# Grouped-query decode attention with an MLP on one core: unrolled chunks of 8192 keys against engine loops over chunks of 16384 keys

## The chip, the core and the metric

The kernel runs on one core of one Trainium2 chip. The metric is device time in microseconds (us); lower is better. A core has a matrix engine (TensorE, in the profile PE, with its weight loads as PEld), a vector engine (VectorE, DVE), a scalar engine (ScalarE, ACT), GpSimd (POOL) and SyncE (SP), which in this kernel issues nearly all loads. Loads from the chip's main memory into the on-chip memory of 128 partitions are carried out by 16 DMA engines.

## The reference

One token goes through attention over a long cache and, in parallel, through an MLP; both are added to the token. All numbers are float32.

```python
x = A_x                                    # 1 x 1 x 512
xn = layernorm(x)
q = (xn @ wq).reshape(32 heads, 128)       # wq: 512 x 4096
# 8 key/value heads, each used by 4 query heads; 65536 keys of 128 numbers
scores = q . k_cache * 128 ** -0.5
o = softmax(scores) . v_cache
out = x + o.reshape(4096) @ wo + relu(xn @ w1) @ w2    # w1: 512 x 1792, w2: 1792 x 512
```

The two caches have 8 x 65536 x 128 numbers each, 268 MB each. With the weights (wq and wo of 8.4 MB each, w1 and w2 of 3.7 MB each) about 561 MB are read, and 2 KB are written.

## The kernel before

The program is fully unrolled in Python and recorded by a tile framework, which adds the semaphores and assigns buffers out of pools. It goes head by head (`h`, 8 heads with their 4 queries), and within a head first over 8 chunks of 8192 keys (`score_chunk`), then over the same 8 chunks of values (`value_chunk`).

All loads stand in one queue, SyncE's, in the order in which the code is written. A chunk of keys (line 84) is one DMA of 128 rows of 32 KB, one for each partition; a chunk of values (line 93) likewise, but the very last one comes in seven pieces (`LAST`). Keys and values share a pool of four places (`kv`, 32 KB in each partition), so a load waits until the chunk four loads before it has been used. The weights come in pieces of 1 MB from a pool of four (`wpool`, line 77), and their loads stand between the chunks: the part of wq for the next head, w1 and w2 in quarters during the first heads, wo for the head during its values. The last quarter of w2 (line 313) comes in two pieces after the last values.

- Scores (line 166): four matmuls, one for each group of 32 output partitions, make 2048 scores in one bank of PSUM. VectorE transposes that in blocks of 32 x 32 (line 171), ScalarE copies the four used columns of 32 (line 173), and after a chunk VectorE takes its maximum (line 174).
- Softmax (lines 182 to 197): once per head, after all its keys. The maxima go through a transpose on TensorE (line 184), a reduction, a small diagonal matrix (line 188) and a matmul that spreads them to all partitions (line 190), and ScalarE computes the exponentials of the whole head in four instructions, one per query, with their sums.
- Values (line 213): each matmul takes the probabilities of four times 128 keys as weights and 4 x 128 columns of values, into one accumulator per head (`acc_o`); in the last head one times 128.
- Output of a head (lines 246 to 254, then 236): the accumulator is copied, summed over its four blocks with the normalisation (`norm`), and multiplied by this head's part of wo into `acc_y`. This is done while the next head's second chunk of keys is due.
- MLP (lines 268 and 236): pieces of it stand between chunks of the first heads.
- End: after the last values come the output of the last head, the last quarter of w2, an addition of x (line 319) and the store (line 320).

Of the kernel before, what the change touches and what calls it, by code (L numbers as in the profile page):

```python
# [8 lines left out]
F32 = mybir.dt.float32  # L9
# [3 lines left out]
PSUM = bass.MemoryType.PSUM  # L13
# [3 lines left out]
HQ, HKV, DH = 32, 8, 128  # L17
SK = 65536
DFF = 1792
G = HQ // HKV  # L20
# [3 lines left out]
KEYS = CT * TW  # L24
CHUNK = 8192
NCH = SK // CHUNK
TPC = CHUNK // KEYS
NB = CHUNK // P
LAST = {NCH - 1: [16, 16, 8, 8, 8, 4, 4]}
WIDE = 4  # L30
A = D // P
FB = DFF // P
EPS = 1e-5
# [3 lines left out]
def attention_and_mlp_kernel(  # L37
# [10 lines left out]
):  # L48

    nc = tc.nc
    scale = float(DH) ** -0.5

    const = ctx.enter_context(tc.tile_pool(name="const", bufs=1))
    kv = ctx.enter_context(tc.tile_pool(name="kv", bufs=4))  # L60
    wpool = ctx.enter_context(tc.tile_pool(name="wpool", bufs=4))
    work = ctx.enter_context(tc.tile_pool(name="work", bufs=2))
    ps_s = ctx.enter_context(tc.tile_pool(name="ps_s", bufs=3, space=PSUM))
    ps_a = ctx.enter_context(tc.tile_pool(name="ps_a", bufs=1, space=PSUM))
    ps_m = ctx.enter_context(tc.tile_pool(name="ps_m", bufs=2, space=PSUM))


    xT = const.tile([P, A], F32, name="xT")
    nc.scalar.dma_start(xT, x.rearrange("(p a) -> p a", p=P))
    x4 = const.tile([P, P], F32, name="x4")  # L70

    weights = {}

    def load(name, src):
        w = wpool.tile([P, 4, 512], F32, name="w")
        n, m = src.shape[1], src.shape[2]
        nc.sync.dma_start(w[:, :n, :m], src)  # L77
        weights[name] = w

    chunks = {}  # L80

    def load_k(h, n):
        t = kv.tile([P, CHUNK], F32, name="kv")
        nc.sync.dma_start(t, k[h, n])  # L84
        chunks["k", h, n] = t

    def load_v(h, n):
        t = kv.tile([P, CHUNK], F32, name="kv")
        src = v[h, n * CHUNK : (n + 1) * CHUNK, :].rearrange("(p b) d -> p (b d)", p=P)
        b = 0  # L90
        for nb in LAST.get(n, [NB]) if h == HKV - 1 else [NB]:
            cut = slice(b * DH, (b + nb) * DH)
            nc.sync.dma_start(t[:, cut], src[:, cut])
            b += nb
        chunks["v", h, n] = t

    load(("q", 0), wq[0])


    ident = const.tile([P, P], F32, name="ident")  # L100
    make_identity(nc, ident)
    ones = const.tile([P, P], F32, name="ones")
    nc.vector.memset(ones, 1.0)

    sel = const.tile([P, WIDE, G], F32, name="sel")
    places = [ident[:, 32 * c : 32 * c + WIDE * G].rearrange("p (b g) -> p b g", g=G) for c in range(CT)]
    nc.vector.tensor_add(sel, places[0], places[1])
    nc.vector.tensor_add(sel, sel, places[2])
    nc.vector.tensor_add(sel, sel, places[3])
    nc.vector.memset(x4, 0.0)  # L110
    qpad = [const.tile([P, 32], F32, name=f"qpad{i}") for i in range(2)]
    for t in qpad:
        nc.vector.memset(t, 0.0)
    acc_o = [ps_a.tile([P, 512], F32, name=f"acc_o{i}") for i in range(2)]
    for t in acc_o:
        nc.vector.memset(t, 0.0)  # L116
    acc_y = ps_a.tile([P, 512], F32, name="acc_y")
    nc.vector.memset(acc_y[:, :P], 0.0)


    st = const.tile([P, 8], F32, name="st")
    xc = const.tile([P, A], F32, name="xc")
    sq = const.tile([P, A], F32, name="sq")
    xn = const.tile([P, A], F32, name="xn")
    nc.vector.reduce_sum(st[:, 0:1], xT, axis=AX.X)
    pm = ps_m.tile([P, 512], F32, name="pm")
    nc.tensor.matmul(pm[:, 0:1], ones, st[:, 0:1], start=True, stop=True)
    nc.vector.tensor_scalar_mul(st[:, 1:2], pm[:, 0:1], 1.0 / D)
    nc.vector.tensor_scalar(xc, xT, st[:, 1:2], None, op0=ALU.subtract)
    nc.vector.tensor_mul(sq, xc, xc)  # L130
    nc.vector.reduce_sum(st[:, 2:3], sq, axis=AX.X)
    pm = ps_m.tile([P, 512], F32, name="pm")
    nc.tensor.matmul(pm[:, 0:1], ones, st[:, 2:3], start=True, stop=True)
    nc.vector.tensor_scalar(st[:, 3:4], pm[:, 0:1], 1.0 / D, EPS, op0=ALU.mult, op1=ALU.add)
    nc.scalar.activation(st[:, 4:5], st[:, 3:4], AF.Sqrt)
    nc.vector.reciprocal(st[:, 5:6], st[:, 4:5])

    nc.vector.tensor_mul(st[:, 6:7], st[:, 5:6], st[:, 5:6])
    nc.vector.tensor_mul(st[:, 6:7], st[:, 6:7], st[:, 3:4])
    nc.vector.tensor_scalar(st[:, 6:7], st[:, 6:7], -0.5, 1.5, op0=ALU.mult, op1=ALU.add)  # L140
    nc.vector.tensor_mul(st[:, 7:8], st[:, 5:6], st[:, 6:7])
    nc.vector.tensor_scalar_mul(xn, xc, st[:, 7:8])  # L142

    def queries(h):
        w = weights.pop(("q", h))
        pq = ps_m.tile([P, 512], F32, name="pm")
        for g in range(G):
            for a in range(A):
                nc.tensor.matmul(  # L149
                    pq[:, g : g + 1], w[:, a, g * DH : (g + 1) * DH], xn[:, a : a + 1],  # L150
                    start=(a == 0), stop=(a == A - 1),
                )
        nc.vector.tensor_copy(qpad[h % 2][:, :G], pq[:, :G])  # L153

    scores, chunk_max, probs, part_sum = {}, {}, {}, {}

    def score_chunk(h, n):
        t = chunks.pop(("k", h, n))
        if n == 0:
            scores[h] = work.tile([P, NCH * NB, G], F32, name="scores")  # L160
            chunk_max[h] = work.tile([P, G, NCH], F32, name="chunk_max")
        for s in range(TPC):
            pt = ps_s.tile([P, TW], F32, name="pt")
            for c in range(CT):
                lo = (s * CT + c) * TW
                nc.tensor.matmul(  # L166
                    pt[32 * c : 32 * c + 32, :], qpad[h % 2], t[:, lo : lo + TW],
                    start=True, stop=True,
                )
            tr = work.tile([P, SUB, 32], F32, name="tr", bufs=3)  # L170
            nc.vector.transpose(tr.rearrange("p b i -> p (b i)"), pt)  # L171
            b0 = n * NB + s * SUB
            nc.scalar.copy(scores[h][:, b0 : b0 + SUB, :], tr[:, :, :G])  # L173
        nc.vector.reduce_max(  # L174
            chunk_max[h][:, :, n],
            scores[h][:, n * NB : (n + 1) * NB, :].rearrange("p b g -> p g b"),
            axis=AX.X,
        )

    def softmax(h):  # L180
        m = work.tile([P, G], F32, name="m")
        nc.vector.reduce_max(m, chunk_max.pop(h), axis=AX.X)  # L182
        pm = ps_m.tile([P, 512], F32, name="pm")
        nc.tensor.transpose(pm[:G, :P], m, ident)  # L184
        mg = work.tile([G, 1], F32, name="mg")
        nc.vector.reduce_max(mg, pm[:G, :P], axis=AX.X)
        dg = work.tile([G, G], F32, name="dg")
        nc.vector.tensor_scalar(dg, ident[:G, :G], mg, -scale, op0=ALU.mult, op1=ALU.mult)  # L188
        pb = ps_m.tile([P, 512], F32, name="pm")
        nc.tensor.matmul(pb[:, :G], ones[:G, :], dg, start=True, stop=True)  # L190
        bias = work.tile([P, G], F32, name="bias")
        nc.vector.tensor_copy(bias, pb[:, :G])  # L192
        probs[h] = work.tile([P, NCH * NB, G], F32, name="probs")
        part_sum[h] = work.tile([P, G], F32, name="part_sum")
        s = scores.pop(h)
        for g in range(G):
            nc.scalar.activation(  # L197
                probs[h][:, :, g], s[:, :, g], AF.Exp, bias=bias[:, g : g + 1], scale=scale,
                accum_out=part_sum[h][:, g : g + 1],
            )  # L200

    def wide(h):


        return 1 if h == HKV - 1 else WIDE

    def value_chunk(h, n):
        t = chunks.pop(("v", h, n))
        w = wide(h)
        for i in range(NB // w):  # L210
            c = i % CT
            b = n * NB + i * w
            nc.tensor.matmul(  # L213
                acc_o[h % 2][32 * c : 32 * c + w * G, : w * DH],
                probs[h][:, b : b + w, :].rearrange("p b g -> p (b g)"),
                t[:, i * w * DH : (i + 1) * w * DH],
                start=(n == 0 and i < CT), stop=(n == NCH - 1 and i >= NB // w - CT),
            )

    norm = {}  # L220

    def totals(h):

        pm = ps_m.tile([P, 512], F32, name="pm")
        nc.tensor.matmul(pm[:, :G], ones, part_sum.pop(h), start=True, stop=True)  # L225
# [124 lines left out]
```

## Time and profile before

| | |
|---|---|
| median of 3 runs | 1320.74 us (1320.47 to 1320.99) |
| profiled execution, first to last instruction (its span; the profile gives no other time of it) | 1318.7 us |
| median of the runs less this span | 2.0 us |
| read from main memory | 560.99 MB, 425 GB/s over the span |
| granted TensorE clock, mean | 0.752 of full speed |

How to read the profile: busy times are those of each engine and can overlap. The chain that ended last goes back from the last instruction, at each step to what released it. A group's line has the line of code, engine, operation, output and inputs, shapes and count, then busy time and the mean of one in ns, then the idle time just before and what ended it. A line of the timeline has the start, the duration, the instruction and, in brackets, the idle time before it. A line of the windows has the stretch, its length, the busy time of PE, PEld, DVE, ACT and POOL with counts, the granted clock, the mean share of time in which the 16 DMA engines were busy, and GB/s. A line of the DMA queues has packets, MB, and the time of the packets as a share of 16 engines' span. A float32 matmul counts as two instructions on PE and two on PEld.

### The profile page before, as it was taken

Reading aid. Unit: us, or ns where it says so; the run is one execution under the profiler, and the core shown is the slowest. Engines: PE = TensorE matmul, PEld = TensorE weight load, DVE = VectorE, ACT = ScalarE, POOL = GpSimd, SP = SyncE. Lnnn points to the kernel's source line nnn. Section 1 sums busy time; section 2 is a strip of 40 time slices with the busy share of each in tenths; the row PEclk is TensorE's granted clock in tenths of the full one; section 3 lists DMA queues with packets and bytes.
Section 4 is the critical chain, followed back from the end, with each engine's and each line's share of the span. In section 5 each row is a group of like instructions: output and inputs, shape, how many; then the busy total and the mean of one; then the engine's idle time right before and its main releaser. Section 6 shows DMA issues by size and latency. Waiting matters only on the chain.

```text
span 1318.7 us, 12826 instructions
## 1 busy us (share of the span) xinstructions
PE 782.5 (59%) x5702; PEld 261.2 (20%) x5702; DVE 245.4 (19%) x440; ACT 103.5 (8%) x323; POOL 0.7 (0%) x6
## 2 busy tenths in 40 slices
PE   5554676446665466664675556664665644665655
PEld 3211212112121121211211112111121110221244
DVE  3330013300133001330013300233002320023200
ACT  1011000110001100101001110002000120001200
POOL 0000000000000000000000000000000000000000
PEclk9767877877778767667778777767777677777677
DMA  9999999999999999999999999999999999999997
GB/s 399 428 436 430 431 432 425 432 428 432 430 427 430 429 433 429 429 429 430 429 431 432 431 434 431 430 429 429 429 429 435 435 430 431 429 429 430 430 431 289
DMA packets 24646, 561.81 MB, mean 426 GB/s; under 512 B 2696, under 2 KB 3216, under 8 KB 5648
## 3 DMA queue, kind: packets, MB, share of 16 engines
q1 hardware_dynamic: 24448, 561.00, 99.3%
q8 instruction: 44, 0.72, 0.2%
q14 instruction: 10, 0.08, 0.0%
q10 hardware_dynamic: 144, 0.00, 0.0%
HBM read 560.99 MB, written 0.00 MB: 425 GB/s over the span
## 4 chain that ended last, share of the span: by engine, by line
DMA 84%; PE 14%; ACT 0%; DVE 0%; issue 0%; SPq 0%; ACTq 0%; DVEq 0%
DMA kv<-v 43%; DMA kv<-k 42%; PE pt L166 7%; PE acc_o L213 7%; ACT probs L197 0%; PE acc_y L236 0%; DVE acc_o L116 0%; DVE tr L171 0%; SPq L77 0%; DVE chunk_max L174 0%; PE pm L190 0%; PE pm L225 0%; PE pm L252 0%; SPq L84 0%; SPq L287 0%
## 5 line engine op out<-in xcount | busy, mean ns | idle before, releaser
L166 PE MATMUL pt<-kv,qpad 128*32 128x512 f32 x2048 | 361.6, 870 | 233.5 <-DMA kv<-k 233.2
L213 PE MATMUL acc_o<-kv,probs 128*16 128x512 f32 (+1 forms) x2816 | 338.1, 650 | 218.8 <-DMA kv<-v 218.8
L171 DVE STREAM_TRANSPOSE tr<-pt 128x512 f32<-128x512 f32 x256 | 183.5, 717 | 380.4 <-PE pt L166 375.9
L166 PEld LDWEIGHTS pt<-kv,qpad 128*32 128x32 f32 x2048 | 95.9, 152 | 490.6 <-issue 482.8
L213 PEld LDWEIGHTS acc_o<-kv,probs 128*16 128x16 f32 (+1 forms) x2816 | 90.1, 117 | 451.3 <-DMA kv<-v 255.1
L173 ACT COPY scores<-tr 128x64 f32<-128x64 f32 x256 | 62.4, 244 | 1114.2 <-DVE tr L171 1114.2
L153 DVE COPY qpad<-pm 128x4 f32<-128x4 f32 x8 | 1.3, 163 | 398.9 <-PE pm L149 398.9
L174 DVE TENSOR_REDUCE chunk_max<-scores 128x4 f32<-128x256 f32 x64 | 38.5, 601 | 18.6 <-ACT scores L173 18.6
L246 DVE COPY o<-acc_o 128x512 f32<-128x512 f32 (+1 forms) x8 | 5.1, 642 | 190.5 <-PE acc_o L213 190.5
L197 ACT ACTIVATE probs<-scores,bias 128x512 f32<-128x512 f32 x32 | 37.7, 1180 | 18.5 <-DVE bias L192 18.5
L149 PE MATMUL pm<-xn,w 128*128 128x1 f32 x256 | 36.3, 276 | 1.7 <-DVE xn L142 1.7
L149 PEld LDWEIGHTS pm<-xn,w 128*128 128x128 f32 x256 | 35.6, 226 | 8.0 <-issue 6.2
L225 PE MATMUL pm<-part_sum,ones 128*128 128x4 f32 x16 | 4.7, 364 | 42.5 <-ACT probs L197 42.5
L268 PEld LDWEIGHTS pm<-xn,w 128*128 128x128 f32 x112 | 14.0, 206 | 3.5 <-issue 3.5
L268 PE MATMUL pm<-xn,w 128*128 128x1 f32 x112 | 14.3, 262 | 0.0
L225 PEld LDWEIGHTS pm<-part_sum,ones 128*128 128x128 f32 x16 | 4.0, 310 | 43.2 <-ACT probs L197 43.2
L184 PE MATMUL pm<-ident,m 128*4 128x128 f32 x8 | 2.3, 284 | 16.4 <-DVE m L182 16.4
L236 PE MATMUL acc_y<-w,oT 128*1 128x128 f32 x256 | 10.6, 316 | 2.0 <-DVE oT L254 2.0
L252 PE MATMUL pm<-norm,o 128*128 128x4 f32 x58 | 7.8, 256 | 6.2 <-DVE o L246 6.2
L227 DVE RECIPROCAL r<-pm 128x4 f32<-128x4 f32 x8 | 1.5, 183 | 45.9 <-PE pm L225 45.9
L252 PEld LDWEIGHTS pm<-norm,o 128*128 128x128 f32 x58 | 7.1, 191 | 13.9 <-DVE o L246 13.9
L190 PE MATMUL pm<-dg,ones 4*128 4x4 f32 x16 | 4.3, 335 | 5.0 <-DVE dg L188 5.0
(47 smaller groups left out, 45.1 us busy)
## 6 DMA issues: line engine op xcount, KB each, us to landing
kv<-k SPq DMA_DIRECT2D x64, 4096.0 KB, 34.3
kv<-v SPq DMA_DIRECT2D x63, 4096.0 KB, 35.1
w<-wq SPq DMA_DIRECT2D x8, 1024.0 KB, 40.3
w<-wo SPq DMA_DIRECT2D x8, 1024.0 KB, 35.2
w<-w SPq DMA_DIRECT2D x6, 1024.0 KB, 34.8
kv<-v SPq DMA_DIRECT2D x2, 1024.0 KB, 26.4
kv<-v SPq DMA_DIRECT2D x3, 512.0 KB, 29.6
w<-w SPq DMA_DIRECT2D x1, 512.0 KB, 34.4
```

The costliest lines, as they stand in the source:

```text
L149: nc.tensor.matmul(pq[:, g : g + 1], w[:, a, g * DH : (g + 1) * DH], xn[:, a : a + 1], start=(a == 0), stop=(a == A - 1),)
L166: nc.tensor.matmul(pt[32 * c : 32 * c + 32, :], qpad[h % 2], t[:, lo : lo + TW], start=True, stop=True,)
L171: nc.vector.transpose(tr.rearrange("p b i -> p (b i)"), pt)
L173: nc.scalar.copy(scores[h][:, b0 : b0 + SUB, :], tr[:, :, :G])
L174: nc.vector.reduce_max(chunk_max[h][:, :, n], scores[h][:, n * NB : (n + 1) * NB, :].rearrange("p b g -> p g b"), axis=AX.X,)
L197: nc.scalar.activation(probs[h][:, :, g], s[:, :, g], AF.Exp, bias=bias[:, g : g + 1], scale=scale, accum_out=part_sum[h][:, g : g + 1],)
L213: nc.tensor.matmul(acc_o[h % 2][32 * c : 32 * c + w * G, : w * DH], probs[h][:, b : b + w, :].rearrange("p b g -> p (b g)"), t[:, i * w * ...
L225: nc.tensor.matmul(pm[:, :G], ones, part_sum.pop(h), start=True, stop=True)
L236: nc.tensor.matmul(acc_y[32 * c : 32 * c + 1, :P], lhsT, row[:, c * P : (c + 1) * P], start=first[0], stop=last,)
L246: nc.vector.tensor_copy(o[:, :n, :].rearrange("p b d -> p (b d)"), acc_o[h % 2][:, : n * DH])
L252: nc.tensor.matmul(pm[:, :G], o[:, b, :], r[:, b, :], start=(b == 0), stop=(b == n - 1))
L268: nc.tensor.matmul(pm[:, j : j + 1], w[:, a, j * P : (j + 1) * P], xn[:, a : a + 1], start=(a == 0), stop=(a == A - 1),)
```

## The change

The program is rewritten without the tile framework's buffers and semaphores. TensorE, ScalarE and VectorE each run a loop of their own (32 turns on TensorE and ScalarE; 8 turns of four parts on VectorE), with semaphores that the code names; `take` waits until a semaphore has reached a count and takes that count off it. SyncE's loads are written out.

All heads form one stream of 32 chunks of 16384 keys, four for each head. There is one place for keys (`kt`) and one for values (`vt`), of 64 KB in each partition; a load is a DMA of 128 rows of 64 KB. Loads go in the order keys, values, keys, values; a load of keys waits until the keys before it have been scored, a load of values until the values before it have been used. The maximum is a running one: each chunk has its own small chain through TensorE and VectorE, its exponentials are taken against the running maximum, and the earlier sum and output are scaled by `corr`. The output of a chunk is reduced to four columns and added to `o_run`; after four parts it goes into `oT`.

All of wq comes first, into the place of the values, and w1 into a place of its own (`wt`); all 32 queries and the hidden layer are computed before the loop, with the token as the weights of the matmuls and single rows as output. wo and w2 come after the last values in four pieces each, wo into the place of the keys. The same layout of the inputs in memory is kept, apart from the sizes of the pieces.

The core of the diff; the whole of the functions before stands above, and the setup, the layer norm and the computing of the queries and the hidden layer are left out:

```diff
+CHUNK = 16384
+V_CUTS = 4
+WO_CUTS = [8, 8, 8, 8]
+W2_CUTS = [6, 4, 2, 2]
+def take(e, sem, n=1):
+    return e.sem_inc(sem, -n).wait_op(sem, n, "sem-ge")
...
+    for i in range(2):
+        cut = slice(i * half, (i + 1) * half)
+        sp.dma_start(vt[:, cut], wq_row[:, cut]).then_inc(sem(f"wq{i}"), 16)
+    sp.dma_start(wt, w1_row).then_inc(sem("w1"), 16)
+    for n in range(NCH):
+        if n:
+            sp.wait_ge(sem("kfree"), n)
+        sp.dma_start(kt, k[0, n]).then_inc(sem("k"), 16)
+        sp.wait_ge(sem("vfree"), n + 1)
+        src = v[0, n * CHUNK : (n + 1) * CHUNK, :].rearrange("(p b) d -> p (b d)", p=P)
+        step = CHUNK // V_CUTS
+        for i in range(V_CUTS):
+            if n < NCH - 1 and i:
+                sp.sem_inc(sem(f"v{i}"), 16)
+                continue
+            cut = slice(i * step, (i + 1) * step) if n == NCH - 1 else slice(0, CHUNK)
+            sp.dma_start(vt[:, cut], src[:, cut]).then_inc(sem(f"v{i}"), 16)
+    sp.wait_ge(sem("kfree"), NCH)
...
+        sp.dma_start(kt[:, cut], wo_row[:, cut]).then_inc(sem(f"wo{i}"), 16)
...
+    sp.wait_ge(sem("wfree"), 1)
...
+        sp.dma_start(wt[:, cut], w2_row[:, cut]).then_inc(sem(f"w2{i}"), 16)
...
+    with pe.Fori(0, NCH):
+        take(pe, sem("q"))
+        take(pe, sem("k"), 16)
         for s in range(TPC):
-            pt = ps_s.tile([P, TW], F32, name="pt")
+            take(pe, sem("free"))
             for c in range(CT):
                 lo = (s * CT + c) * TW
-                nc.tensor.matmul(
-                    pt[32 * c : 32 * c + 32, :], qpad[h % 2], t[:, lo : lo + TW],
+                last = pe.matmul(
+                    bank[s % BANKS][32 * c : 32 * c + 32, :], qpad, kt[:, lo : lo + TW],
                     start=True, stop=True,
                 )
+            last.then_inc(sem("score"), 1)
+        take(pe, sem("m"))
+        pe.transpose(pma[:GROUP, :P], m, ident).then_inc(sem("mT"), 1)
+        take(pe, sem("dg"))
+        pe.matmul(pmb[:, :GROUP], ones[:GROUP, :], dg, start=True, stop=True).then_inc(sem("nb"), 1)
+        take(pe, sem("probs"))
+        n = NB // WIDE
+        for i in range(n):
+            if i % (n // V_CUTS) == 0:
+                take(pe, sem(f"v{i // (n // V_CUTS)}"), 16)
+            c = 32 * (i % CT)
+            b = i * WIDE
+            last = pe.matmul(
+                acc[c : c + WIDE * GROUP, :],
+                probs[:, b : b + WIDE, :].rearrange("p b g -> p (b g)"),
+                vt[:, b * DH : (b + WIDE) * DH],
+                start=(i < CT), stop=(i >= n - CT),
+            )
+        last.then_inc(sem("acc"), 1)
+        pe.matmul(pma[:, 256 : 256 + GROUP], ones, part_sum, start=True, stop=True)
+        take(pe, sem("o"))
+        for b in range(WIDE):
+            last = pe.matmul(
+                pma[:, 264 : 264 + GROUP], o_sb[:, b, :], sel[:, b, :],
+                start=(b == 0), stop=(b == WIDE - 1),
+            )
+        last.then_inc(sem("part"), 1)
+    with act.Fori(0, NCH):
+        take(act, sem("bias"))
+        act.activation(corr, diff, AF.Exp)
+        for g in range(GROUP):
+            last = act.activation(
+                probs[:, :, g], tr[:, :, g], AF.Exp, bias=nb_new[:, g : g + 1], scale=scale,
+                accum_out=part_sum[:, g : g + 1],
+            )
+        last.then_inc(sem("probs"), 1)
+    with dve.Fori(0, HEADS) as h:
+        for part in range(PARTS):
+            for s in range(TPC):
+                take(dve, sem("score"))
+                if s == TPC - 1:
+                    dve.nop().then_inc(sem("kfree"), 1)
+                dve.transpose(
+                    tr[:, s * SUB : (s + 1) * SUB, :].rearrange("p b i -> p (b i)"), bank[s % BANKS]
+                ).then_inc(sem("free"), 1)
+            dve.drain()
+            dve.reduce_max(m, tr.rearrange("p b i -> p i b")[:, :GROUP, :], axis=AX.X).then_inc(sem("m"), 1)
...
+            take(dve, sem("mT"))
+            then(dve.reduce_max(mg, pma[:GROUP, :P], axis=AX.X))
+            dve.tensor_scalar(dg, ident[:GROUP, :GROUP], mg, -scale, op0=ALU.mult, op1=ALU.mult).then_inc(sem("dg"), 1)
+            take(dve, sem("nb"))
+            then(dve.tensor_tensor(nb_new, pmb[:, :GROUP], nb_run, op=ALU.min))
+            then(dve.tensor_sub(diff, nb_new, nb_run))
+            dve.tensor_copy(nb_run, nb_new).then_inc(sem("bias"), 1)
+            take(dve, sem("acc"))
+            dve.nop().then_inc(sem("vfree"), 1)
+            dve.tensor_copy(o_sb.rearrange("p b d -> p (b d)"), acc).then_inc(sem("o"), 1)
+            take(dve, sem("part"))
+            dve.tensor_mul(l_run, l_run, corr)
+            then(dve.tensor_mul(o_run, o_run, corr))
...
+    for i, n in enumerate(WO_CUTS):
+        pe.wait_ge(sem(f"wo{i}"), 16)
+        for j in range(lo, lo + n):
...
+            last = pe.matmul(
+                y4[c : c + 1, :], oT[:, j : j + 1], kt[:, j * D : (j + 1) * D],
+                start=(j < CT), stop=(j >= NQ - CT),
+            )
...
+    for i, n in enumerate(W2_CUTS):
+        pe.wait_ge(sem(f"w2{i}"), 16)
+        for b in range(lo, lo + n):
+            for c in range(CT):
+                last = pe.matmul(
+                    yacc[32 * c : 32 * c + 1, :P], hcol[:, b : b + 1],
+                    wt[:, b * D + c * P : b * D + (c + 1) * P], start=False, stop=(b == FB - 1),
+                )
...
+    dve.tensor_copy(ysb, yacc[:, :P]).then_inc(sem("y"), 1)
```

More of the change, by code (lines that the diff above doesn't have):

```diff
@@ L87, in load_v @@
[L87 to L101, printed above, removed]
@@ L127, in attention_and_mlp_kernel @@
[L127 to L134, printed above, removed]
@@ L135, in attention_and_mlp_kernel @@
[L135 to L148, printed above, removed]
-                nc.tensor.matmul(
[L150 to L161, printed above, removed]
+    ctx.enter_context(tc.tile_critical(no_gpsimd_drain=True))
+    def sbuf(name, *shape):
+        return nc.alloc_sbuf_tensor(name, list(shape), F32).ap()
+    def psum(name):
+        return nc.alloc_psum_tensor(name, [P, 512], F32).ap()
@@ new lines, in attention_and_mlp_kernel, with sem @@
+    sems = {}
+    def sem(name):
+        if name not in sems:
+            sems[name] = nc.alloc_semaphore(name)
+        return sems[name]
+    kt = sbuf("kt", P, CHUNK)
+    vt = sbuf("vt", P, CHUNK)
+    wt = sbuf("wt", P, FB * D)
+    tr = sbuf("tr", P, NB, 32)
+    probs = sbuf("probs", P, NB, GROUP)
+    o_sb = sbuf("o_sb", P, WIDE, DH)
+    rows = sbuf("rows", P, 3, 512)
+    ysum = sbuf("ysum", P, 512)
+    ident = sbuf("ident", P, P)
+    ones = sbuf("ones", P, P)
+    sel = sbuf("sel", P, WIDE, GROUP)
@@ new lines, in attention_and_mlp_kernel @@
+    pe.wait_ge(sem("zero"), 1)
+    pe.wait_ge(sem("xn"), 1)
+    for a in range(XA):
+        if a % 2 == 0:
+            pe.wait_ge(sem(f"wq{a // 2}"), 16)
+        for h in range(HEADS):
+            c = 32 * (h % CT)
+            last = pe.matmul(
+                bank[h // CT][c : c + 1, :], xn[:, a : a + 1],
+                vt[:, a * HEADS * 512 + h * 512 : a * HEADS * 512 + (h + 1) * 512],
+                start=(a == 0), stop=(a == XA - 1),
+            )
+    last.then_inc(sem("qrow"), 1)
@@ new lines, in attention_and_mlp_kernel @@
+    last.then_inc(sem("hrow"), 1)
+    dve.wait_ge(sem("hrow"), 1)
+    dve.nop().then_inc(sem("wfree"), 1)
+    dve.tensor_scalar_max(rows[:, 2, :], bank[2], 0.0).then_inc(sem("rows"), 1)
+    pe.wait_ge(sem("rows"), 2)
+    for b in range(4):
+        last = pe.matmul(
+            pmb[:, b * CT : (b + 1) * CT], rows[:, 2, b * P : (b + 1) * P], selq, start=True, stop=True
+        )
+    last.then_inc(sem("hT"), 1)
+    dve.wait_ge(sem("hT"), 1)
+    dve.tensor_copy(
+        hT.rearrange("p c b -> p b c"), pmb[:, : 4 * CT].rearrange("p (b c) -> p b c", c=CT)
+    ).then_inc(sem("free"), BANKS)
@@ L168, in score_chunk @@
                     start=True, stop=True,
                 )
[L170 to L199, printed above, removed]
-            )
@@ L202, in wide @@
[L202 to L217, printed above, removed]
-            )
@@ L220, in attention_and_mlp_kernel @@
[L220 to L225, printed above, removed]
-        r = work.tile([P, G], F32, name="r")
-        nc.vector.reciprocal(r, pm[:, :G])
-        norm[h] = work.tile([P, WIDE, G], F32, name="norm")
-        for b in range(wide(h)):
-            nc.vector.tensor_mul(norm[h][:, b, :], sel[:, b, :], r)
-    first = [True]
-    def project(lhsT, row, last=False):
-        for c in range(CT):
-            nc.tensor.matmul(
-                acc_y[32 * c : 32 * c + 1, :P], lhsT, row[:, c * P : (c + 1) * P],
-                start=first[0], stop=last,
-            )
-        first[0] = False
```

304 lines of the change are left out of this document (175 added, 129 removed).

## The prediction

> **What bounds the kernel now.** I read the page's busy shares, slices and queues first, then the chain that ended last, then the instructions of the stretch in which the chain is cleanest, and the end of the run by windows.
>
> ```profile
> span 1318.7 us, 12826 instructions
> PE 782.5 (59%) x5702; PEld 261.2 (20%) x5702; DVE 245.4 (19%) x440; ACT 103.5 (8%) x323; POOL 0.7 (0%) x6
> ...
> GB/s 399 428 436 430 431 432 425 432 428 432 430 427 430 429 433 429 429 429 430 429 431 432 431 434 431 430 429 429 429 429 435 435 430 431 429 429 430 430 431 289
> DMA packets 24646, 561.81 MB, mean 426 GB/s; under 512 B 2696, under 2 KB 3216, under 8 KB 5648
> ...
> q1 hardware_dynamic: 24448, 561.00, 99.3%
> q8 instruction: 44, 0.72, 0.2%
> ...
> DMA 84%; PE 14%; ACT 0%; DVE 0%; issue 0%; SPq 0%; ACTq 0%; DVEq 0%
> ```
>
> The 16 DMA engines are occupied for 99.3% of the span, and every slice but the first and the last moves 425 to 436 GB/s. TensorE is busy 59%, and the 14% that it has in the chain are matmuls that free a place for a load. So the bound is reading 561 MB at the engines' own pace, and only four things can move the time: what each packet costs beside its bytes, other traffic on these engines, the uneven end, and the work behind the last byte.
>
> ```profile
> 1191.94 5.34 PE L166 MATMUL pt<-kv,qpad 128*32 128x512 f32 x32 [4.38 <-DMA kv<-k]
> 1201.65 5.88 PE L166 MATMUL pt<-kv,qpad 128*32 128x512 f32 x32 [4.38 <-DMA kv<-k]
> 1211.37 6.14 PE L166 MATMUL pt<-kv,qpad 128*32 128x512 f32 x32 [3.85 <-DMA kv<-k]
> ```
>
> In these TensorE instructions each chunk of 8192 keys starts when its DMA lands, 9.71 us after the one before (1201.65 - 1191.94, 1211.37 - 1201.65): 4.19 MB in 9.71 us is 432 GB/s. Its 16 score matmuls (32 in the trace, each float32 matmul counting twice) take 5.34 to 6.14 us, and TensorE then idles some 4 us.
>
> **The change, term by term.** The sum starts from the span of 1318.7 us; the median of the runs, 1320.74, is 2.0 above it, for what lies around the first and last instruction, and I keep these 2.0. The bytes stay as they are: the same weights and caches are read once each.
>
> *Packets.* From the diff, the changed kernel's rows of 128 partitions are 32 key loads (4096), 31 whole value loads and four quarters (4480), wq in two, w1 in one, wo and w2 in four pieces each (1408): 9984 rows. The small packets of before, 2696 under 512 B, are nearly 16 for each of some 160 loads, so the 79 loads of after bring some 1264. That makes 11,250 packets in place of 24,448: 825 fewer on each of 16 engines. What does one cost beside its bytes? The best slice moves 436 GB/s, at which 4.19 MB would take 9.62 us; the chunk takes 9.71, with nine packets on each engine (eight rows and the completion): 0.09/9, or 10 ns. From below it is nothing (the best slice may be a matter of counting). From above: 99.3% of the span is 1309.5 us, 561.00 MB at 436 GB/s are 1286.7 us, and the 22.8 us between, over 24,448/16 = 1528 packets, are 14.9 ns. I take 10, as the clean chunks are nearest to what is removed: 825 x 10 ns = **-8.2 us**, between 0 and -12.3.
>
> *Code.* The 0.72 MB of instruction traffic are 63 bytes for each of 2 x 5702 TensorE instructions: this is TensorE's unrolled program. The changed program writes its 71 matmuls of a turn once in a loop, and has 158 outside, so 229 x 4 = 916 such instructions. What the traffic costs shows at the end:
>
> ```profile
> 1300.00:1302.00 2.00, 0.00 (x0) 0.00 (x0) 0.00 (x0) 0.00 (x0) 0.00 (x0) 0.95 0.86 349
> 1302.00:1304.00 2.00, 1.28 (x28) 0.90 (x32) 0.00 (x0) 0.00 (x0) 0.00 (x0) 0.50 0.90 345
> 1304.00:1306.00 2.00, 2.00 (x44) 1.42 (x40) 0.00 (x0) 0.00 (x0) 0.00 (x0) 0.50 0.77 311
> 1306.00:1308.00 2.00, 2.00 (x44) 1.36 (x40) 0.00 (x0) 0.00 (x0) 0.00 (x0) 0.50 0.78 279
> 1308.00:1310.00 2.00, 2.00 (x71) 1.66 (x64) 0.00 (x0) 0.00 (x0) 0.00 (x0) 0.85 0.54 215
> 1310.00:1312.00 2.00, 2.00 (x83) 1.79 (x76) 0.00 (x0) 0.00 (x0) 0.00 (x0) 1.00 0.52 200
> 1312.00:1314.00 2.00, 1.31 (x30) 0.57 (x21) 0.33 (x2) 0.00 (x0) 0.00 (x0) 1.00 0.19 67
> ```
>
> (Last two columns: the DMA engines' share, and GB/s.) From 1300 us on some engines are done and others are not: the idle shares, 0.14 to 0.81 of 2 us, add up to 4.9 us. Every load has 128 rows for 16 engines, which I take to be eight each; so what makes some late is traffic that is not spread evenly, and code is the only such traffic of size. With the 0.72 MB themselves (1.7 us at 430 GB/s) the code costs up to 6.6 us; nothing, if the last pieces' own waits make the unevenness. 8% of it stays if each block is fetched once. I take **-5.5 us**, between 0 and -6.6; code that is fetched again in each turn is a rival.
>
> *The end.*
>
> ```profile
> 1314.94 0.43 PEld L236 LDWEIGHTS acc_y<-w,hT 128*1 128x1 f32 x16
> 1315.05 0.62 PE L236 MATMUL acc_y<-w,hT 128*1 128x128 f32 x16
> 1315.74 0.29 DVE L319 TENSOR_TENSOR y<-acc_y,x 128x128 f32<-128x128 f32 x1 [1.61 <-PE acc_y L236]
> 1316.05 0.59 SPq L320 DMA_DIRECT2D y<-y  x1
> ```
>
> Now the last bytes come at some 1313.6 (67 GB/s in the last window with traffic), 5.1 us before the end, since the last head's output and its rows of wo come between. After, the last bytes are two blocks of w2: 8 matmuls (16 instructions, 0.62), a copy (0.29), the store (0.59 and 2.06 to the end) and three hand-overs of some 0.1 make 3.9 us. **-1.0 us**, between +0.5 and -1.5.
>
> Of the work that moves in front of it: the rows of wo take 32 matmuls, of which the last 8 stand behind the last quarter of wo. That lands with 3.67 MB of w2 still to come, 8.5 us at 432 GB/s; 8 matmuls at a third of a microsecond each (5.34/16) and a copy take under 4 us. Without that cover they would cost those 4 us.
>
> *One place each.* This is what must hold for the bound to stay. A load of 16384 keys takes 19.42 us (2 x 9.71), a turn 38.84. Key loads and value loads alternate in one queue, and a load is issued when its place is free.
>
> ```profile
> L171 DVE STREAM_TRANSPOSE tr<-pt 128x512 f32<-128x512 f32 x256 | 183.5, 717 | 380.4 <-PE pt L166 375.9 <-ACT scores L173 2.0
> L174 DVE TENSOR_REDUCE chunk_max<-scores 128x4 f32<-128x256 f32 x64 | 38.5, 601 | 18.6 <-ACT scores L173 18.6
> L197 ACT ACTIVATE probs<-scores,bias 128x512 f32<-128x512 f32 x32 | 37.7, 1180 | 18.5 <-DVE bias L192 18.5
> L197 ACT ACTIVATION_READ_ACCUMULATOR probs<-scores,bias 128x1 f32 x32 | 6.0, 187 | 0.0
> L190 PE MATMUL pm<-dg,ones 4*128 4x4 f32 x16 | 4.3, 335 | 5.0 <-DVE dg L188 5.0
> L246 DVE COPY o<-acc_o 128x512 f32<-128x512 f32 x7 | 4.8, 692 | 124.6 <-PE acc_o L213 124.6
> L184 PE MATMUL pm<-ident,m 128*4 128x128 f32 x8 | 2.3, 284 | 16.4 <-DVE m L182 16.4
> L186 DVE TENSOR_REDUCE mg<-pm 4x1 f32<-4x128 f32 x8 | 2.2, 279 | 3.1 <-PE pm L184 3.1
> L188 DVE TENSOR_SCALAR dg<-ident,mg 4x4 f32<-4x4 f32 x8 | 1.7, 217 | 0.3
> L192 DVE COPY bias<-pm 128x4 f32<-128x4 f32 x8 | 1.3, 163 | 5.0 <-PE pm L190 5.0
> ```
>
> From the keys' landing (zero): scores end at 10.7 to 12.3 (two times 5.34 to 6.14). The key place is free, and the next key load issued a microsecond later, at 13.3; the value load keeps the engines busy until 19.42. Spare: 6 us. Then the chain of one running maximum: transpose 0.72, a maximum over twice the elements 1.2, transpose on TensorE 0.28, 0.28, 0.22, two passes of 0.34, three operations of 0.16 on 4 columns, one exponential of 4 columns 0.2, and four of 128 columns, a quarter of 1.18 and 0.19 each: 5.9 us, with hand-overs 6.5. Probabilities stand at 18.8, and the values land at 19.42: hidden, by 0.6 us; what more it takes delays the values' matmuls, which have spare themselves.
>
> ```profile
> 1110.45 5.44 PE acc_o L213 x32
> ...
> 1152.99 6.35 PE acc_o L213 x32
> ```
>
> By these pieces of the chain, twice 5.44 to 6.35: values are used up at 32.1 at the latest, and the next value load is issued at 33.1, against the keys' end at 38.84. Spare: 5.7 us. TensorE itself ends its turn with the sum (two passes, 0.7), the wait for the copy of acc (0.69) and four small matmuls (8 instructions, 0.4, since 16 took 0.62 above): 33.9, a spare of 4.9 us before the next keys. Where a turn starts late, it no longer waits for the values (12.3 + 6.5 + 12.7 + 1.8 = 33.3 us of work), so 5.5 us per turn can be lost before TensorE sets the pace. Behind a value load that waits on SP's queue stands the next key load, whose place comes free later than the values' before it: no added wait. The waits of VectorE for the weighted sum hold up only the next transposes, and these come after the next landing. Cost taken: **0**, from 0 (nothing here moves bytes faster) up to the rival below.
>
> The sum: 1318.7 - 8.2 - 5.5 - 1.0 = 1304.0, and with the 2.0 around it **1306.0 us**.
>
> **Rivals.** *(a) The row of 64 KB goes as two packets.* The trace has no packet over 32 KB to show otherwise. 8064 packets come back, 504 per engine: 5.0 us of the 8.2, so 1311.
>
> *(b) Code is fetched again in every turn, hidden.* The body is 304 instructions, 71 x 4 and 20 others: 19 KB, and code comes in blocks of 16.4 KB (0.72 MB / 44), so it lies on two. Two blocks in each of 31 jumps back are 62, against 44 now: the code costs 6.6 x 62/44 = 9.3 instead of 6.6, so 2.7 more in place of 5.5 less, 1314.2; 1318 if packets are worth half. The trace cannot say whether a block once run is kept: the program before never jumps. By the Trainium skill, "Runtime: NRT & Kernel Launch", Instruction fetch mechanics, the fetch is sequential and a jump to a target outside the present window of two pages forces a fetch before it goes on; the same section gives TensorE a memory of 2048 instructions, into which this body would fit.
>
> *(c) The same, and it stalls TensorE: slower.* Place: the jump back, after the last small matmul of a turn, with the next keys' scores behind it. The nearest row for a small transfer beside full queues is this:
>
> ```profile
> xT<-x ACTq DMA_DIRECT2D x1, 2.0 KB, 5.3
> ```
>
> It decides from 5.5 us per turn, so 5.3 stands just short of it. Behind a row of 64 KB in place of one of 32 KB (9.71/8 = 1.2 us) it would be 6.5: 1.0 x 31 = 31 us on top of the 1314.2 of (b), 1345. A stall of 5.9 us gives 1327. For it: the body exceeds a block. Against it: the spare, and that TensorE's fetches of now are never seen to stop it.
>
> *(d) Rows at a pitch of 64 KB read slower.* At 32 KB the pace is 432 GB/s, so nothing of it shows in this trace. Each 1% would cost 13 us; 2% make the forecast 1332. By the Trainium skill, "DMA: Bandwidth & Descriptors", Latency and other measured facts, copies at a row pitch of a large power of two slow down, from 207 GB/s at 512 KiB to 103 at 4 MiB, against 214 in full; no run here shows it, and 64 KB lies below the smallest pitch listed.
>
> **How the numbers follow.** Forecast 0.52 (1301 to 1310), (a) 0.09, (b) 0.17, (c) 0.13, (d) 0.05, other losses 0.04. About 0.2%, 2.6 us, can be told from no change. The upper part of (b) is no change: 0.05. Faster 0.72, slower 0.23. Low end: 1318.7 - 12.3 - 6.6 - 1.5 + 2.0, 1300.3, taken as 1301; high end 1330, which takes in (a), (b) and the lower part of (c), and leaves out some 0.15 above and 0.03 below.
>
> **What would show it.** Right: some 11,000 packets on the load queue, key loads landing 38.7 us apart, a chain nearly all DMA, a handful of instruction fetches, engines ending within 2 us of each other, and less than 4 us behind the last bytes. Wrong: over 60 instruction fetches (b); score matmuls that start well after their keys have landed, with idle that ends on TensorE's own queue (c); twice the packets (a); slices under 428 GB/s with loads always queued (d); or idle DMA engines in the middle of the run, if a place comes free too late.

## The result, and the profile after

| | before | after |
|---|---|---|
| median of the runs | 1320.70 us (1320.47 to 1320.99, 4 runs) | 1306.03 us (1305.98 to 1306.09, 4 runs) |
| span of the profiled execution | 1318.7 us | 1304.3 us |
| granted TensorE clock, mean | 0.752 | 0.726 |

The ratio is 0.9886, with a 95% interval from 0.9872 to 0.9900: 14.7 us less.

The page after, in the lines that answer to those of before (slices, packets, queues, chain):

```profile
span 1304.3 us, 12331 instructions
...
GB/s 402 449 421 442 422 442 424 444 424 434 434 432 436 424 444 424 444 424 444 424 444 424 444 422 444 424 444 422 446 422 444 422 440 428 434 434 430 438 419 344
DMA packets 11398, 561.07 MB, mean 430 GB/s; under 512 B 1400, under 2 KB 1408, under 8 KB 1664
...
q1 hardware_dynamic: 11240, 561.00, 99.5%
q8 instruction: 3, 0.05, 0.0%
...
DMA 3%; SPq 0%; PE 0%; issue 0%; DVE 0%; DVEq 0%
DMA wt<-w 3%; SPq L153 0%; SPq L159 0%; PE bank L396 0%; DVE ysb L410 0%; DVEq L341 0%
```

11,240 packets on the load queue, where 11,250 were counted, so a row of 64 KB is one packet; and three instruction fetches in place of 44. The chain is short because it cannot be followed back through the loops' semaphores: where it breaks off, the profile names no releaser, and the waits there appear as those of an engine's own queue. For the same reason the idle time in the next lines, TensorE's in two turns, ends on "PEq":

```profile
633.45 8.84 PE L291 MATMUL bank<-kt,qpad 128*32 128x512 f32 x64 [9.03 <-PEq L48]
652.65 9.46 PE L307 MATMUL acc<-vt,probs 128*16 128x512 f32 x64 [6.46 <-PEq L48]
672.15 9.96 PE L291 MATMUL bank<-kt,qpad 128*32 128x512 f32 x64 [7.91 <-PEq L48]
691.35 8.88 PE L307 MATMUL acc<-vt,probs 128*16 128x512 f32 x64 [5.24 <-PEq L48]
710.86 9.38 PE L291 MATMUL bank<-kt,qpad 128*32 128x512 f32 x64 [8.50 <-PEq L48]
```

A turn takes 38.70 us (672.15 - 633.45, 710.86 - 672.15), against 4 x 9.71 = 38.84 at the pace of before, and before each batch TensorE is idle for 5 to 9 us. Before the keys all of that is waiting; before the values its first part goes to the chain of the maximum and the exponentials. That it waits for data and not for code is seen from SyncE's side. These are its two load issues of one turn:

```profile
642.61 0.33 SPq L139 DMA_DIRECT2D kt<-k  x1
...
662.32 0.33 SPq L148 DMA_DIRECT2D vt<-v  x1
```

The next keys are asked for 10.0 us before the values on their way are used (652.65), the next values 9.8 us before the next keys are (672.15). In this turn the DMA engines always have a load queued, and over the whole run the packets of the load queue take 99.5% of their time. The windows of the end:

```profile
1294.00:1296.00 2.00, 1.66 (x28) 0.63 (x24) 0.69 (x1) 0.00 (x0) 0.00 (x0) 0.55 0.99 403
1296.00:1298.00 2.00, 1.39 (x52) 0.96 (x47) 0.00 (x0) 0.00 (x0) 0.00 (x0) 1.00 0.97 387
1298.00:1300.00 2.00, 1.57 (x48) 0.93 (x40) 0.00 (x0) 0.00 (x0) 0.00 (x0) 1.00 0.21 86
1300.00:1302.00 2.00, 0.62 (x16) 0.31 (x16) 0.29 (x1) 0.00 (x0) 0.00 (x0) 1.00 0.00 0
```

The share of the DMA engines stays at 0.97 until 1298 and is gone by 1300; before, it fell off over 14 us. What comes behind the last bytes:

```profile
1300.35 0.62 PE L396 MATMUL bank<-wt,hT 128*1 128x128 f32 x16 [0.60 <-DMA wt<-w]
1301.03 0.29 DVE L410 COPY ysb<-bank 128x128 f32<-128x128 f32 x1 [5.66 <-PE bank L396]
1301.35 0.67 SPq L162 DMA_DIRECT2D y<-ysb  x1
```

From 1300.35 to the end at 1304.3 are 4.0 us. By the times of the packets in the traces, the last data are in at 1299.9, and were in at 1313.5 before: 4.4 us to the end, against 5.2.

### The profile page after: what moved, and what is told of

It is laid out like the page before. It is cut to its first block, busy times and chain, and to the rows that moved or that the text cites. A ratio compares the mean times of both kernels' runs of the same rounds, so it can differ in the third digit from the quotient of the medians.

```text
span 1304.3 us, 12331 instructions
## 1 busy us (share of the span) xinstructions
PE 692.2 (53%) x4828; PEld 217.6 (17%) x4828; DVE 297.3 (23%) x677; ACT 72.6 (6%) x291; POOL 0.7 (0%) x6
## 3 DMA queue, kind: packets, MB, share of 16 engines
q1 hardware_dynamic: 11240, 561.00, 99.5%
## 5 line engine op out<-in xcount | busy, mean ns | idle before, releaser
L291 PE MATMUL bank<-kt,qpad 128*32 128x512 f32 x2048 | 296.3, 743 | 268.8 <-PEq L48 268.8
L307 PE MATMUL acc<-vt,probs 128*16 128x512 f32 x2048 | 295.0, 741 | 189.6 <-PEq L48 189.6
L342 DVE STREAM_TRANSPOSE tr<-bank 128x512 f32<-128x512 f32 x256 | 183.4, 717 | 385.5 <-DVEq L48 369.6
L291 PEld LDWEIGHTS bank<-kt,qpad 128*32 128x32 f32 x2048 | 81.0, 133 | 457.8 <-issue 457.8
L307 PEld LDWEIGHTS acc<-vt,probs 128*16 128x16 f32 x2048 | 69.5, 113 | 388.4 <-issue 388.4
L329 ACT ACTIVATE probs<-tr,nb_new 128x128 f32<-128x128 f32 x128 | 63.7, 507 | 0.0
L317 PE MATMUL pma<-sel,o_sb 128*128 128x4 f32 x256 | 32.8, 252 | 25.4 <-PEq L48 25.4
L317 PEld LDWEIGHTS pma<-sel,o_sb 128*128 128x128 f32 x256 | 31.0, 191 | 27.2 <-issue 27.2
L346 DVE TENSOR_REDUCE m<-tr 128x4 f32<-128x512 f32 x32 | 32.2, 1005 | 2.9
L299 PE MATMUL pmb<-dg,ones 4*128 4x4 f32 x64 | 14.7, 297 | 30.1 <-PEq L48 30.1
L329 ACT ACTIVATION_READ_ACCUMULATOR probs<-tr,nb_new 128x1 f32 x128 | 23.9, 186 | 0.0
L314 PE MATMUL pma<-part_sum,ones 128*128 128x4 f32 x64 | 12.3, 263 | 0.0
```

The source lines that it names most:

```text
L291: last = pe.matmul(bank[s % BANKS][32 * c : 32 * c + 32, :], qpad, kt[:, lo : lo + TW], start=True, stop=True,)
L299: pe.matmul(pmb[:, :GROUP], ones[:GROUP, :], dg, start=True, stop=True).then_inc(sem("nb"), 1)
L307: last = pe.matmul(acc[c : c + WIDE * GROUP, :], probs[:, b : b + WIDE, :].rearrange("p b g -> p (b g)"), vt[:, b * DH : (b + WIDE) * DH], ...
L314: pe.matmul(pma[:, 256 : 256 + GROUP], ones, part_sum, start=True, stop=True)
L317: last = pe.matmul(pma[:, 264 : 264 + GROUP], o_sb[:, b, :], sel[:, b, :], start=(b == 0), stop=(b == WIDE - 1),)
L329: last = act.activation(probs[:, :, g], tr[:, :, g], AF.Exp, bias=nb_new[:, g : g + 1], scale=scale, accum_out=part_sum[:, g : g + 1],)
```

## The experiments

The theory is the prediction's: the bound stays the loads, and the gain is packets, code and the end, with the single places at no cost. Each term was put back, or taken alone. Where nothing else is said, a kernel is the changed one with the edit shown, and differences are against 1306.03 us.

**Packets.** Two pieces for each load, then four; TensorE waits for all of them.

```diff
-        sp.dma_start(kt, k[0, n]).then_inc(sem("k"), 16)
+        for i in range(2):
+            cut = slice(i * (CHUNK // 2), (i + 1) * (CHUNK // 2))
+            sp.dma_start(kt[:, cut], k[0, n][:, cut]).then_inc(sem("k"), 16)
...
-        take(pe, sem("k"), 16)
+        take(pe, sem("k"), 32)
```

(and the values likewise)

> The changed kernel with every load of keys and values cut into two of 32 KB rows. 8064 rows and 63 x 16 completions come back, 9072 packets, 567 on each engine. Theory (a packet costs some 10 ns beside its bytes): +5.7 us, 1311.7, and a turn of 38.87 in place of 38.70 us between key landings. Rival (packets are free, the whole gain is code and end): 1306.0 and 38.70. Second rival (what helps is that a load is long, not that its rows are): the same +5.7, but then four pieces of 16 KB rows would not cost three times as much.

> The changed kernel with every load of keys and values cut into four of 16 KB rows: 24192 rows and 189 x 16 completions more, 1701 packets on each engine. Theory (10 ns a packet): +17.0 us, 1323.0, three times what two pieces cost. Rival (packets are free): 1306.0.

Measured: 1310.78 us with two (+4.75), 1320.39 with four (+14.36). The rise is 3.02 times as large for three times the packets: 4.75/567 = 8.4 ns and 14.36/1701 = 8.4 ns each, the same from 64 KB down to 16 KB. By itself this does not say that the packets are what costs: the DMAs were multiplied in step with them (63 and 189 more, each with nine packets on each engine), so a price for each DMA, as in the second rival, would have come out the same. The durations of the packets in the traces tell the two apart. In the median a row of 64 KB takes 2421 ns, one of 32 KB 1218 and one of 16 KB 614, so two halves take 15 ns longer than the whole and four quarters 35 ns; a completion takes 9 ns. That is rather more than the 8.4 ns of the whole runs, and leaves nothing for the length of a DMA. Two batches of scores with four pieces, and that kernel's load queue:

```profile
640.56 10.03 PE L294 MATMUL bank<-kt,qpad 128*32 128x512 f32 x64 [11.14 <-PEq L48]
679.66 9.26 PE L294 MATMUL bank<-kt,qpad 128*32 128x512 f32 x64 [9.56 <-PEq L48]
```

```profile
q1 hardware_dynamic: 38456, 561.01, 100.0%
```

Between these two lie 39.10 us. In the mean of the 31 turns from the first batch of scores to the last, a turn takes 38.72 us in the changed kernel, 38.86 with two pieces and 39.18 with four. With 16 KB rows all of the change's gain but 0.3 us is given back, although loops, places and end are the new ones.

**Rows alone, in the kernel before.**

```diff
-CHUNK = 8192
+CHUNK = 16384
-LAST = {NCH - 1: [16, 16, 8, 8, 8, 4, 4]}
+LAST = {NCH - 1: [64, 16, 16, 8, 8, 8, 4, 4]}
-    kv = ctx.enter_context(tc.tile_pool(name="kv", bufs=4))
+    kv = ctx.enter_context(tc.tile_pool(name="kv", bufs=2))
```

(and the small loads moved to chunks that still exist)

> The kernel before with the rows alone changed: chunks of 16384 keys, two places of 64 KB in the shared pool in place of four of 32 KB, the last value load in eight pieces. 567 packets less on each engine. Theory (packets at 10 ns): -5.7 us, 1315.0, the rest of the change's gain absent. Rival (two places are too few, or the loops are what makes them enough): not below 1320.7.

Measured: 1316.91 us, 3.9 less than the 1320.83 of the kernel before beside it. At 8.4 ns 567 packets are 4.8; the 0.9 that is missing was not followed up. Two places shared by keys and values are enough in the unrolled program too: the loops are not what makes them enough.

**Code.** TensorE's loop written out.

```diff
-    with pe.Fori(0, NCH):
+    for _ in range(NCH):
```

> The changed kernel with TensorE's loop written out 32 times; nothing else changes. 304 instructions x 32 are 38 blocks of code to fetch, against 44 in the kernel before. Theory (code traffic is what makes the engines end unevenly): +4.7 us, 1310.8, between 0 and +5.7, with some 40 instruction fetches and engines that end over 4 us apart. Rival (the uneven end came from the waits of the last pieces): 1306.0, with an even end in spite of the fetches.

Measured: 1311.73 us, +5.7: the top of the range. Its queues and the end:

```profile
q1 hardware_dynamic: 11240, 561.00, 99.2%
q8 instruction: 40, 0.66, 0.2%
```

```profile
1297.90:1299.90 2.00, 2.00 (x20) 0.38 (x16) 0.00 (x0) 0.00 (x0) 0.00 (x0) 0.62 0.93 383
1299.90:1301.90 2.00, 1.42 (x32) 0.69 (x28) 0.69 (x1) 0.00 (x0) 0.00 (x0) 0.52 0.54 227
1301.90:1303.90 2.00, 1.61 (x61) 1.17 (x56) 0.00 (x0) 0.00 (x0) 0.00 (x0) 1.00 0.47 193
1303.90:1305.90 2.00, 1.28 (x42) 0.67 (x32) 0.00 (x0) 0.00 (x0) 0.00 (x0) 1.00 0.31 121
```

Nothing differs but the 37 more fetches, and the uneven end is back: half of the engines' time is idle from 1299.9 on, as before the change. That the waits of the last pieces make it falls. In the mean a fetch costs 5.7/37 = 0.15 us, though all of them are 0.61 MB, 1.4 us at 430 GB/s.

The loss shows at the end, but it is not made there: the last batch of scores already starts at 1258.51, against 1252.78 in the changed kernel. It is made in steps. Of the 31 turns four take 39.92 to 39.95 us, and the others 38.6 to 39.0; the four make 4.8 of the 5.7 us. The first of the four lies between these two batches:

```profile
284.81 8.65 PE L291 MATMUL bank<-kt,qpad 128*32 128x512 f32 x64 [7.52 <-PEq L48]
324.73 5.74 PE L291 MATMUL bank<-kt,qpad 128*32 128x512 f32 x32 [9.31 <-PEq L48]
```

The trace has 40 fetch packets, of 16 KB and 1.07 us each in the median, and the 9th, 17th, 25th and 33rd of them stand in just these four turns. That is what would be seen if the fetches went round eight of the 16 engines: each new round makes the latest engine later by about one fetch, and all engines have to be waited for. The trace does not name the engine of a packet, so the going round is inferred.

**How much code is kept.** The loop with four chunks in its body, then eight.

```diff
-    with pe.Fori(0, NCH):
+    with pe.Fori(0, NCH // 4):
+        for _ in range(4):
```

> The changed kernel with four chunks written out in TensorE's loop of 8 turns: 1216 instructions, 4.75 blocks. Theory (code once fetched is kept, up to 2048 instructions): some 7 instruction fetches, each above three worth 0.15 us (5.7 us for 37 of them in the unrolled kernel): 1306.6. Rival (a window of two blocks): nearly all blocks are fetched in each turn, 38, and TensorE may stall besides: 1311.7 or more.

> The changed kernel with eight chunks written out in TensorE's loop of 4 turns: 2432 instructions, 9.5 blocks, over 2048. Theory (2048 instructions are kept): the blocks are fetched again in each turn, some 40 fetches, 1311.7, and a stall at three jumps back, hidden by the spare of TensorE. Rival (more is kept): some 12 fetches, 1307.4.

Measured: 1305.98 us with four, no difference from 1306.03, and 1313.23 with eight, +7.2. The instruction queues of the two:

```profile
q8 instruction: 7, 0.11, 0.0%
```

```profile
q8 instruction: 45, 0.74, 0.2%
```

By the times of these packets, the body of 1216 instructions is fetched once, up to 195 us, and nothing more comes until 1283; that of 2432 is fetched over the whole run, in every turn of its loop. So a loop on TensorE is cheap if its body is short enough to be kept, and past that it can be worse than the unrolled program (1311.73): 45 fetches and not 40. Where between 1216 and 2432 the limit lies, no run shows.

The steps are the same here. With 45 fetches five of the stretches between two batches of scores take 39.85 to 40.00 us, and they are those of the 9th, 17th, 25th, 33rd and 41st fetch: one step more than in the unrolled program, and 1.5 us more time. With seven fetches there is no such stretch, and the 0.6 us expected of four more fetches did not come. So 0.15 us is the mean over many fetches, not the price of a single one; a round of eight costs some 1.2 us.

**The end.** w2 in one piece, and then with one block in the last piece.

```diff
-W2_CUTS = [6, 4, 2, 2]
+W2_CUTS = [14]
```

> The changed kernel with w2 as one piece; the four small matmuls of wo's part stand ahead of it. 56 matmuls instead of 8 stand behind the last bytes. Theory (the end is the work behind the last bytes): 112 instructions at 0.62/16 are 4.3 us instead of 0.62, and 27 packets fewer on each engine give back 0.2: +3.4 us, 1309.4. Rival (the end is bound by the store, the pieces are worth nothing): 1306.0.

Measured: 1311.07 us (1309.79 to 1311.50, 4 runs), +5.0. The 112 instructions behind the last bytes take 6.14 us and not the 4.3 reckoned. The granted clock is 0.50 to 0.54 from 1300.2 to 1306.4 here, where the changed kernel has 1.00 in its last matmuls:

```profile
1300.23 6.14 PE L402 MATMUL bank<-wt,hT 128*1 128x128 f32 x112 [4.26 <-DMA wt<-w]
1306.45 0.29 DVE L409 COPY ysb<-bank 128x128 f32<-128x128 f32 x1 [11.14 <-PE bank L402]
```

6.14 in place of 0.62 makes 5.5, less the packets. The pieces are worth what they keep from standing there.

```diff
-W2_CUTS = [6, 4, 2, 2]
+W2_CUTS = [6, 5, 2, 1]
```

> The changed kernel with w2 in pieces of 6, 5, 2 and 1 block in place of 6, 4, 2 and 2. Theory (the end is the work behind the last bytes): 4 matmuls instead of 8 stand there, 8 instructions fewer at 0.04 to 0.05 us: -0.35 us, 1305.7. Rival (the hand-overs set the end): 1306.0.

Measured: 1305.81 us (1305.68 to 1306.07, 4 runs), against 1305.98 to 1306.09 of the changed kernel in other runs: the right sign and half the size, inside the spread. Not settled, and no version that clearly beats the change was found.

**The spare time of single places.** Useless matmuls at the end of each of TensorE's turns, ahead of the next keys' scores.

```diff
         last.then_inc(sem("part"), 1)
+        for _ in range(5):
+            pe.matmul(y4[0:1, :], ones[:, 0:1], rows[:, 0, :], start=True, stop=True)
```

> The changed kernel with five matmuls of no use (one row of output, 512 columns, into the accumulator of wo's part before that is used) at the end of each of TensorE's turns: 4.3 us at the full clock, 8.6 at half of it. Theory (one place each has spare time): by the changed kernel's trace TensorE works 27.6 us of a turn of 38.7 when it waits for nothing, so nothing: 1306.0. By the prediction's own spare of 5.5 us: +1.0 us a turn if the five take 6.5, some +31. Rival (a place comes free just in time): each microsecond costs 31.

> As with five useless matmuls per turn, but nine. Five took 5.3 us a turn (169.6 us in 32), so nine take 9.5. Theory (27.6 us of TensorE's work in a turn of 38.7, so 11 us to spare): nothing, 1306.0. The prediction's spare of 5.5 us: 4.0 us in each of 31 turns, +125, 1431.

> Fourteen useless matmuls per turn, 14.8 us. Theory (27.6 us of work): 3.7 us too much in each of 31 turns, +115, 1421, and the DMA engines idle in each turn. The prediction's spare: 9.3 us too much, +290, 1596.

Measured: 1306.05 us with five, 1306.10 with nine, 1308.63 (one run) with fourteen. Five do not tell the two reckonings apart. Nine take 8.6 us a turn (276.1 us in 32) and leave the scores 1.75 us shorter (240.3 us in all instead of 296.3), so TensorE has 6.9 us more to do in each turn, at no cost: that refutes the spare of 5.5 us. TensorE with fourteen, in one turn and at the values of the next:

```profile
663.16 11.75 PE L323 MATMUL y<-rows,ones 128*1 128x512 f32 x27
674.32 0.63 PE L291 MATMUL bank<-kt,qpad 128*32 128x512 f32 x3
...
674.77 7.43 PE L291 MATMUL bank<-kt,qpad 128*32 128x512 f32 x61
...
691.28 9.64 PE L307 MATMUL acc<-vt,probs 128*16 128x512 f32 x64 [5.26 <-PEq L48]
...
731.22 8.45 PE L307 MATMUL acc<-vt,probs 128*16 128x512 f32 x64 [3.54 <-PEq L48]
```

The fourteen took 11.8 us here, not 14.8, so the scores start some 2 us late; but they then take 7.9 us (674.32 to 682.20), not 8.4 to 10.0. Of the 5.26 us of idle before the values some 3.5 are the exponentials and what leads to them; in the last line only these 3.54 are left, so in some turns TensorE no longer waits for the values at all. In the mean of 32 turns the fourteen take 12.7 us (406.6 in all), and scores and values 1.6 us less than in the changed kernel. That is 11.1 us more, just the 11 that were reckoned as spare: fourteen bring TensorE to its limit and do not refute the 11. What failed in the forecast of 1421 was to add 14.8 us to a work that stays as it is. The loads lose nothing: their last data are in at 1299.8, as in the changed kernel. The 2.6 us come at the end, where the last turn's fourteen stand ahead of the rows of wo:

```profile
1280.85 11.75 PE L323 MATMUL y<-rows,ones 128*1 128x512 f32 x27
1292.01 0.60 PE L382 MATMUL y<-kt,oT 128*1 128x512 f32 x3
...
1301.37 2.01 PE L398 MATMUL bank<-wt,hT 128*1 128x128 f32 x61
```

The last matmuls end at 1303.38 instead of 1300.97. So the cover of wo's rows is used up there: 2.4 us too much of 11.8.

## Why the prediction was right

It said 1306.0 and 1306.03 was measured. The mechanism is the one that it named: the loads stay the bound, and fewer packets, less code and a shorter end make the gain. But its terms were off in opposite directions, so the match to 0.03 us is luck. In the right column the counts are measured, and the prices are those of the experiments:

| term | predicted | from the runs |
|---|---|---|
| packets: 825 fewer on each engine | -8.2 us, 10 ns each | -6.9, at 8.4 ns |
| code: 44 fetches to 3 | -5.5 | -6.3, 41 at 0.15 us in the mean |
| the end | -1.0 | -0.7 (5.2 to 4.4 us from the last data to the end) |
| sum | -14.7 | -13.9 of 14.7 |

0.8 us of the gain stay without a term.

*Packets.* The count was right to 10 in 11,250. The price came from a comparison with the best slice, 436 GB/s, and that step was unsound: after the change the slices (but for the first and the last) lie between 419 and 449, while the scores start evenly every 38.7 us; with 16 KB rows they lie between 426 and 429. So how far slices differ goes with the size of the packets, and the best slice is no measure of a pace; that it gave 10 and not 15 ns was luck. The bounds 0 and 14.9 held.

*Code.* The term was set below its own bound of 6.6 because the last pieces' waits might have had a share in the uneven end. The unrolled loop shows that they had none worth seeing. The loss shows at the end, as the prediction read it, but it is made on the way there, in steps.

*The end* takes 4.0 us from the last matmuls on, where 3.9 were reckoned, but these matmuls start 0.5 us after the last data (1299.86 to 1300.35), for which the sum had some 0.1. For the rows of wo, the prediction named 8.5 us as their cover and under 4 us as their need; the fourteen useless matmuls confirm that there is a limit, further off: of their 11.8 us, 9.4 were covered.

*One place each.* The cost of 0 was right, the spare was mis-sized: 4.9 to 6 us were reckoned, and the loads are asked for some 10 us early. The step that failed is the doubling of a batch of 16 score matmuls, 5.34 to 6.14 us, into 10.7 to 12.3 for 32; they take 8.4 to 10.0. The windows show why, two of the changed kernel and one of that with fourteen useless matmuls:

```profile
633.45:637.50 4.05, 4.05 (x24) 1.23 (x28) 0.96 (x2) 0.00 (x0) 0.00 (x0) 0.56 0.75 324
637.50:642.00 4.50, 4.50 (x48) 1.22 (x39) 3.74 (x6) 0.00 (x0) 0.00 (x0) 1.00 1.04 451
```

```profile
636.80:645.00 8.20, 7.89 (x67) 2.22 (x65) 5.01 (x7) 0.00 (x0) 0.00 (x0) 1.00 0.94 408
```

After its wait TensorE has a granted clock of 0.56 for the first 4 us, and then 1.00; where it had been kept busy it has 1.00 from the start. The shorter batches of before have the slow start too: that at 1201.65 has a granted clock of 0.50 for 4 us and 0.85 for the rest. Each batch pays the slow start once, so a batch of twice the length takes less than twice the time. The chain of one running maximum was 0.7 us longer than reckoned, by the end of its last exponential in the same turn:

```profile
649.25 0.19 ACT L329 ACTIVATION_READ_ACCUMULATOR probs<-tr,nb_new 128x1 f32 x1
```

From the last score (633.45 + 8.84 = 642.29) to 649.44 are 7.15 us, not 6.5, and the values are used from 652.65, three us later still.

*The rivals.* (a) falls with the packet count. (b) and (c) fall with three fetches, and the long body shows under what condition (b) would have come: 45 fetches and +7.2, where the prediction gave +8.2 for 62. A stall as in (c) showed nowhere: if the 45 fetches of the long body hold up TensorE, it is within its waits for data, since +7.2 us is about what 42 more fetches cost at 0.15 us each (6.5). By the Trainium skill, "Runtime: NRT & Kernel Launch", Instruction fetch mechanics, TensorE's memory takes 2048 instructions, and a jump out of a window of two pages has to fetch; the runs agree with the first figure (1216 kept, 2432 not) and not with a window of two pages of 16 KiB, out of which a body of 4.75 blocks reaches. (d) falls too: at a pitch of 64 KB between rows the 16.8 MB of a turn take 38.70 us, 433 GB/s, no less than the 432 of before. The slowdown by row pitch of the Trainium skill ("DMA: Bandwidth & Descriptors", Latency and other measured facts) does not reach down to that pitch here.

## What to carry to other kernels

Where the DMA engines are busy throughout, count packets and other traffic on them: here 8.4 ns a packet and some 6 us for the instruction fetches made all but some 1.5 of 14.7 us. A second buffer is not needed where each load's wait is shorter than the other stream's transfer; work out when the place comes free, and check it by adding useless work until it hurts, with an eye on what the useful work takes meanwhile. Loop a long unrolled program if the body is short enough to stay in the engine's instruction memory, and order the last loads so that almost nothing stands behind the last one.

## What was not expected of the hardware

- 37 instruction fetches beside full DMA queues cost 5.7 us, four times what their bytes take (0.61 MB, 1.4 us). The cost comes in steps of some 1.2 us, at every eighth fetch after the first, and four fetches more cost nothing where they began no new round of eight.
- A loop body of 1216 instructions on TensorE is kept, one of 2432 is not.
- Useless matmuls between the batches made the useful ones faster: the scores took 7.9 instead of 8.4 to 10.0 us, at a granted clock of 1.00 instead of 0.56 in their first 4 us.
